# Attention keys in three chunks of 128, and the last 64 keys of two head pairs in one score tile (attention and gated MLP on one core)

## Chip, cores and metric

One Trainium2 chip, one core of it. The metric is the device time of one execution in microseconds (us): the median before the change is 725.34 us over 3 runs (722.62 to 725.93). A lower time is better. TensorE's clock has two levels, 1.2 and 2.4 GHz; the profile gives the share of the full one that was granted.

## What is computed

Eight batches, 12 heads of 64, 448 positions. Attention with a sigmoid in place of the softmax, then a gated MLP over 768 features with a product along the positions. Cut to what matters, the reference is:

```
scores = (q @ k.T) / sqrt(64) - log(448)
attn   = sigmoid(scores)
x      = attn @ v                       # heads side by side: (8, 448, 768)
h      = relu(x @ w_in)                 # (8, 448, 1024)
u, g   = h[..., :512], h[..., 512:]
g      = (g - mean(g)) / sqrt(var(g) + 1e-6)
g      = w_spatial @ g + b_spatial      # along the positions
out    = (u * g) @ w_out                # (8, 448, 768)
```

## The kernel before

**Units.** A unit is one batch and one pair of heads (`hp`, 6 per batch), so 48 units. Its q and k arrive as one tile `raw` of 128 partitions (two heads of 64) by 896 columns (448 of k, then 448 of q), its v as 4 chunks of 112 keys. `attention_splits` (L192) makes a high and a low part of `raw` in the tile `qks`: a cast and a subtraction, both on VectorE (DVE), L96 and L97.

**Scores.** A unit's 448 keys are 4 chunks of 112 (`KC`, `NC`). For each chunk `attention_scores` (L200) issues 3 terms (high by high, low by high, high by low) for the 2 heads: 6 matmuls (L207) with 64x112 stationary operands. The two heads lie in the upper and lower 64 rows of the array. ScalarE (ACT) then makes the sigmoid `at` of both heads at once (L212). A score tile takes one of 3 two-bank buffers of PSUM.

**Values.** `attention_values` (L217) multiplies a chunk of v by `at`: 2 matmul calls (L224), plain fp32, with 112x64 stationary operands, one for each head, side by side in the columns of the array. A call runs as two matmuls on the chip, so the profile counts 768 for 384 calls. The sums of a unit's 4 chunks stand in one bank `pav` (2 buffers). At the last chunk ACT copies `pav` to the high part of `x_s` (L96) and DVE makes the low part (L97).

**Order.** `attention(m)` (L372) runs through the 48 chunks of two batches in bursts of 3 (`BURST`): a burst's scores, then the values of the burst before, and so on: 16 bursts of either. The split of unit n+1 is issued ahead of chunk 1 of unit n, the loads of n+2 at chunk 0. Engines run their instructions in the program's order (`in_program_order`), as does the DMA queue of SyncE (SP).

**The rest of a stage.** There are 4 stages of two batches `b0`, `b1`. After the attention: `gate_values` four times (L239, matmuls `pv`), `spatial(b0)` twice (L291, `pg`), `gated(b0)` twice (L317, `pu`), `spatial(b1)` twice, `output(b0)` three times (L341, `po`), `gated(b1)` twice, `output(b1)` three times, between whose parts the first score burst of the next stage is placed. These matmuls are single-pass (fp32r) and write 448 or 512 columns.

**Weights.** In the first stage a generator (`weight_steps`, L136) loads and splits 22 pieces of weights beside the work: 6 of `w_in` (needed by `gate_values`), 4 of `w_sp`, 6 of `w_in` (needed by `gated`), 6 of `w_out` (needed by `output`). `load_weights(n)` runs n of its steps. A piece of `w_in` or `w_out` takes 3 steps (5 DVE operations) or, from piece `NFIRST` = 13 on, 4 steps (4 DVE operations and one more on ACT); then ACT copies the high part (L170) and POOL subtracts for the low part (L171). Attention runs a step after each chunk but chunk 1, from the third burst on; the calls behind `gate_values`, `spatial(b0)`, `gated(b0)` and `spatial(b1)` run `YB` = 4 each. `output` reads block 4 of `w_out` (piece 20) in the last quarter of its first column block.

Of the kernel before, what the change touches and what calls it, by code (L numbers as in the profile page):

```python
# [35 lines left out]
def attn_gmlp_kernel(  # L36
# [20 lines left out]

    nc = tc.nc  # L60
    B, NHP, _, _ = qk.shape
    KC, NC = v.shape[2:4]
    S = out.shape[3]
    D = P // 2
    NCC = out.shape[1]
    DM = NCC * P
    F = w_in.shape[1] // (4 * NCC)
    NFC = F // P
    HALF = 64
    NFULL = 3  # L70
    QK = 1.0 / math.sqrt(D)
    NEG_LOG_S = -math.log(S)
    NT = 2 * S // P
# [12 lines left out]
    x_s = const.tile([P, 2, NCC, 2 * S], F32R, name="x_s")  # L86
    bias_s = const.tile([P, 1], F32, name="bias_s")
# [48 lines left out]
    def weight_steps():  # L136
# [21 lines left out]
        for n, (src, dst, i) in enumerate(steps):  # L158
# [3 lines left out]
            hi, lo = dst[:, i, 0], dst[:, i, 1]  # L162
            scalar = n >= NFIRST
            val = raws.pop(n)
# [18 lines left out]
    loaded = {}  # L183

    def attention_loads(b, hp):
        raw = work.tile([P, 1024], F32, tag="raw", name=f"raw_{b}_{hp}", bufs=4)[:, : 2 * S]
        nc.sync.dma_start(raw, qk[b, hp])
        vt = work.tile([KC, NC, P], F32, tag="v", name=f"v_{b}_{hp}", bufs=4)
        nc.sync.dma_start(vt, v[b, hp])
        loaded[b, hp] = raw, vt  # L190

    def attention_splits(b, hp):  # L192
        raw, vt = loaded[b, hp]
        s = work.tile([P, 2, 2 * S], F32R, tag="split", name=f"qks_{b}_{hp}", bufs=3)
        split(s[:, 0], s[:, 1], raw, nc.vector.tensor_copy)
        loaded[b, hp] = s, vt

    TERMS = ((0, 0), (1, 0), (0, 1))

    def attention_scores(b, hp, c):  # L200
        s = loaded[b, hp][0]
        psc = banks(f"psc_{b}_{hp}_{c}")
        ks = slice(c * KC, (c + 1) * KC)
        for i, (a, e) in enumerate(TERMS):
            for j in range(2):
                rows = slice(j * D, (j + 1) * D)
                nc.tensor.matmul(  # L207
                    psc[:KC, j, :S], s[rows, a, ks], s[rows, e, S:], start=i == 0, stop=i == 2
                )
        at = work.tile([P, 2, 512], F32, tag="big", name=f"at_{b}_{hp}_{c}", bufs=7)  # L210
        at = at[:KC, :, :S]
        nc.scalar.activation(at, psc[:KC, :, :S], AF.Sigmoid, bias=bias_s[:KC], scale=QK)  # L212
        return at

    pav_of = {}

    def attention_values(b, hp, c, at):  # L217
        vt = loaded[b, hp][1]
        if c == 0:
            pav_of[b, hp] = ps_1.tile([P, 512], F32, tag="ps1", name=f"pav_{b}_{hp}")  # L220
        pav = pav_of[b, hp]
        for j in range(2):
            rows = slice(j * D, (j + 1) * D)
            nc.tensor.matmul(  # L224
                pav[rows, :S], vt[:, c, rows], at[:, j], start=c == 0, stop=c == NC - 1
            )
        if c == NC - 1:
            sl = slice((b % 2) * S, (b % 2 + 1) * S)
            split(x_s[:, 0, hp, sl], x_s[:, 1, hp, sl], pav[:, :S], nc.scalar.copy)
# [9 lines left out]
    def gate_values(m, ts):  # L239
# [51 lines left out]
    def spatial(b, fcs):  # L291

        odd = b % 2
        cols = cols_of(b)
        pg = banks(f"pg_{b}_{fcs[0]}")
        for i, fc in enumerate(fcs):
            fs = slice(fc * P, (fc + 1) * P)
            pairs = []
            for c in range(NFULL):
                vn = vns[c + 4 if odd else c]  # L300
                pairs.append(
                    (lambda a, vn=vn: vn[:, a, fs], lambda p, c=c: w_sp_s[:, c, p, cols])
                )
# [61 lines left out]
    BURST = 3  # L365
    units = [(b, hp) for b in range(B) for hp in range(NHP)]

    def ahead(f, n):
        if n < len(units):
            f(*units[n])  # L370

    def attention(m):  # L372

        chunks = [
            (b, hp, c) for b in (2 * m, 2 * m + 1) for hp in range(NHP) for c in range(NC)
        ]
        before = []
        for i in range(0, len(chunks) + BURST, BURST):
            now = []
            for b, hp, c in chunks[i : i + BURST]:  # L380
                n = b * NHP + hp
                if c == 0:
# [6 lines left out]
                now.append((b, hp, c, attention_scores(b, hp, c)))  # L389
# [9 lines left out]
    ahead(attention_loads, 0)  # L399
    ahead(attention_loads, 1)  # L400
    pairs = [(0, 1), (2, 3)]
    running = attention(0)
    for m in range(B // 2):
        for _ in running:
            pass
        for ts in ((0, 1), (2, 3), (4, 5), (6,)):
            gate_values(m, ts)
            load_weights(YB)
        b0, b1 = 2 * m, 2 * m + 1
        for fcs in pairs:  # L410
            spatial(b0, fcs)
            load_weights(YB)
# [6 lines left out]
        for n in range(2):  # L419
            ahead(attention_loads, (m + 1) * 2 * NHP + n)  # L420
# [61 lines left out]
```

## Time and profile before

| what | value |
|---|---|
| median of 3 runs (lowest, highest) | 725.34 us (722.62, 725.93) |
| the profiled execution's own time | 723.27 us |
| its span, first to last instruction | 721.5 us |
| granted TensorE clock, mean | 0.999 of full |
| TensorE matmul busy | 709.3 us, 98% |
| TensorE weight loads busy | 524.2 us, 73% |
| VectorE, ScalarE, GpSimd busy | 280.0, 274.1, 50.3 us |

Busy time of an engine is the union of its instructions. Matmuls are pipelined and their recorded ends are modelled, so a long busy time says that matmuls follow each other without a pause, not that the array is used in full. The chain of waits follows the last instruction back through whatever released each step; its rows give start, length, engine, tile and source line.

### The profile page before, as it was taken

What the parts mean: (1) busy time and instruction counts of PE and PEld (TensorE: products, weight loads), DVE (VectorE), ACT (ScalarE), POOL (GpSimd) and SP (SyncE); (2) the same over time, 40 slices, a digit from 0 to 9 for tenths busy, and PEclk for the clock granted to TensorE, in tenths of its full rate; (3) what the DMA queues carried; (4) which work ended last, traced back from release to release, by engine and by line L of the source; (5) the groups of instructions that cost most, each with busy time, mean ns of one, the idle gap of its engine ahead of it and who ended that gap; (6) DMA issues with size and microseconds to landing.
All of it is one profiled execution on the core that took longest, in us unless ns stands there. A gap on an engine that the chain in (4) does not pass through costs nothing.

```text
span 721.5 us, 9317 instructions
## 1 busy us (share of the span) xinstructions
PE 709.3 (98%) x3928; PEld 524.2 (73%) x3928; DVE 280.0 (39%) x423; ACT 274.1 (38%) x329; POOL 50.3 (7%) x58
## 2 busy tenths in 40 slices
PE   7999999999999999999999999999999999999997
PEld 4554689998755578999865557899985555889996
DVE  4977288703233226320233323722124332362110
ACT  5787322313477721011267771101137775101111
POOL 0333023200000001000000000100000000110000
PEclk9999999999999999999999999999999999999999
DMA  8648012221433200002143320000125320000102
GB/s 265 207 145 275 22 38 89 97 77 38 166 124 119 92 1 1 0 1 77 64 154 118 118 85 1 0 1 26 52 89 167 115 90 1 1 0 1 52 25 77
DMA packets 22938, 55.40 MB, mean 77 GB/s; under 512 B 2288, under 2 KB 8432, under 8 KB 22896
## 3 DMA queue, kind: packets, MB, share of 16 engines
q1 hardware_dynamic: 22896, 54.80, 22.8%
q8 instruction: 31, 0.51, 0.3%
q14 instruction: 11, 0.09, 0.0%
HBM read 43.78 MB, written 11.01 MB: 76 GB/s over the span
## 4 chain that ended last, share of the span: by engine, by line
PE 88%; DVE 2%; ACT 1%; issue 0%
PE pav L224 17%; PE pu L235 16%; PE pv L235 16%; PE po L235 15%; PE psc L207 14%; PE pg L235 10%; DVE gs L97 1%; DVE g L334 1%; ACT gs L96 1%; DVE qks L97 0%; ACT osb L362 0%; DVE wval L109 0%; DVE wval L125 0%; DVE wval L128 0%; DVE qks L96 0%
## 5 line engine op out<-in xcount | busy, mean ns | idle before, releaser
L212 ACT ACTIVATE at<-psc,bias_s 112x896 f32<-112x896 f32 x192 | 181.2, 1009 | 61.4 <-PE psc L207 60.9
L224 PE MATMUL pav<-at,v 112*64 112x448 f32 x768 | 157.6, 547 | 0.0
L207 PEld LDWEIGHTS psc<-qks 64*112 64x112 f32 x1152 | 98.6, 174 | 61.1 <-ACT at L212 17.6
L207 PE MATMUL psc<-qks 64*112 64x448 f32 x1152 | 136.9, 378 | 6.1 <-DVE qks L96 4.7
L235 PE MATMUL po<-gs,w_out_s 128*128 128x448 f32 x576 | 121.4, 369 | 1.6 <-DVE gs L97 1.6
L235 PE MATMUL pu<-x_s,w_in_s 128*128 128x448 f32 x576 | 118.0, 365 | 0.0
L235 PEld LDWEIGHTS po<-gs,w_out_s 128*128 128x128 f32 x576 | 107.4, 188 | 14.1 <-DVE gs L97 3.2
L235 PE MATMUL pv<-w_in_s,x_s 128*128 128x512 f32 x504 | 115.4, 390 | 0.0
L235 PEld LDWEIGHTS pu<-x_s,w_in_s 128*128 128x128 f32 x576 | 108.2, 188 | 8.6
L235 PEld LDWEIGHTS pv<-w_in_s,x_s 128*128 128x128 f32 x504 | 94.3, 188 | 22.3 <-issue 2.8
L224 PEld LDWEIGHTS pav<-at,v 112*64 112x64 f32 x768 | 49.8, 136 | 80.6 <-issue 78.9
L97 DVE TENSOR_TENSOR x_s<-pav,x_s 128x448 fp32r<-128x448 f32 x48 | 29.9, 624 | 147.5 <-ACT x_s L96 147.5
L235 PE MATMUL pg<-w_sp_s,vn 128*128 128x448 f32 x352 | 72.8, 365 | 0.0
L235 PEld LDWEIGHTS pg<-w_sp_s,vn 128*128 128x128 f32 x352 | 65.9, 187 | 5.8
L334 DVE SCALAR_TENSOR_TENSOR g<-pu,g 128x896 f32<-128x896 f32 x16 | 17.4, 1090 | 131.2 <-PE pu L235 131.2
L362 ACT COPY osb<-po 128x896 f32<-128x896 f32 x24 | 21.9, 911 | 116.5 <-PE po L235 116.5
L96 ACT CAST gs<-g 128x896 fp32r<-128x896 f32 x16 | 15.1, 945 | 127.2 <-DVE g L334 127.2
L97 DVE TENSOR_TENSOR qks<-raw,qks 128x896 fp32r<-128x896 f32 x48 | 53.4, 1112 | 1.6
L255 ACT ACTIVATE rv<-pv 128x1024 f32<-128x1024 f32 (+1 forms) x16 | 14.7, 920 | 83.5 <-PE pv L235 83.5
L96 DVE CAST qks<-raw 128x896 fp32r<-128x896 f32 x48 | 30.4, 633 | 40.8 <-PE po L235 34.8
L262 POOL TENSOR_SCALAR rstd<-mv 128x2 f32<-128x2 f32 (+1 forms) x16 | 6.4, 403 | 502.5 <-DVE mv L260 502.5
L259 DVE BATCH_NORM_STATS2 stats<-rv 128x6 f32<-128x512 f32 x28 | 19.0, 679 | 46.9 <-ACT rv L255 46.9
(29 smaller groups left out, 231.1 us busy)
## 6 DMA issues: line engine op xcount, KB each, us to landing
raw<-qk_dram SPq DMA_DIRECT2D x48, 448.0 KB, 4.1
v<-v_dram SPq DMA_DIRECT2D x48, 224.0 KB, 2.8
out_dram<-osb SPq DMA_DIRECT2D x24, 448.0 KB, 2.6
wraw<-w_in_dram SPq DMA_DIRECT2D x12, 512.0 KB, 4.9
wraw<-w_out_dram SPq DMA_DIRECT2D x6, 512.0 KB, 3.6
wraw<-w_sp_dram SPq DMA_DIRECT2D x4, 256.0 KB, 2.5
b_bc<-b_sp_dram SPq DMA_DIRECT2D x1, 256.0 KB, 3.3
```

The source lines that it names most:

```text
L96: copy(hi, src)
L97: nc.vector.tensor_sub(lo, src, hi.bitcast(F32))
L207: nc.tensor.matmul(psc[:KC, j, :S], s[rows, a, ks], s[rows, e, S:], start=i == 0, stop=i == 2)
L212: nc.scalar.activation(at, psc[:KC, :, :S], AF.Sigmoid, bias=bias_s[:KC], scale=QK)
L224: nc.tensor.matmul(pav[rows, :S], vt[:, c, rows], at[:, j], start=c == 0, stop=c == NC - 1)
L235: nc.tensor.matmul(ps, st, mv, start=start and i == 0, stop=stop and i == len(ops) - 1)
L255: nc.scalar.activation(rv[:, :n], pv[:, :n], AF.Relu)
L259: nc.vector.bn_stats(stats, rv[:, i])
L262: nc.gpsimd.tensor_scalar_add(rstd[:, :n], mv[:, :n, 1], 1e-6)
L334: nc.vector.scalar_tensor_tensor(g, pu[:, :, :S], 0.0, g, op0=ALU.max, op1=ALU.mult)
L362: nc.scalar.copy(osb, po[:, :, :S])
```

## The change

Keys are cut into 3 full chunks of 128 and one short one of 64. Two units (`hp` even and odd, a pair of units) share their short chunks: 7 score tiles (`t` = 0 to 6) in place of 8, of which `t` = 3 is the shared one, the even unit's keys in its upper 64 partitions and the odd unit's in its lower 64.

- The shared score tile takes 12 matmuls: 6 for each unit, with 64x128 stationary operands of which 64 columns are keys and 64 are zeros, so that both units' terms add up in one tile. For this `qks` gets 64 more columns, behind the 896 in an even unit and ahead of them in an odd one, which POOL sets to zero in each unit (a `memset` of 128x2x64, 48 in all). All other score matmuls are 64x128 as well.
- In the shared tile's values, 4 calls take 64x64 tiles: rows 0 to 63 (even unit) into one `pav`, rows 64 to 127 (odd unit) into the other. The other tiles take 128x64.
- v is loaded once for a pair of units, 128 partitions by 7x128, 2 buffers (before: each unit, 4 buffers).
- Splits: the odd unit's is issued ahead of `t` = 1, the next pair's even one ahead of `t` = 5.
- `NFIRST` is 11; a step of weights follows each tile but `t` = 1 and 5; `spatial(b1)` runs 8 steps each.

```
+    PART = 2 * S + HALF
-    NFIRST = NCC + NFC + 3
+    NFIRST = NCC + NFC + 1
...
     def attention_splits(b, hp):
+        s = work.tile([P, 2, PART], F32R, tag="split", name=f"qks_{b}_{hp}", bufs=3)
+        odd = hp % 2
+        zeros = s[:, :, :HALF] if odd else s[:, :, 2 * S :]
+        nc.gpsimd.memset(zeros.bitcast(F32), 0.0)
+        body = s[:, :, HALF:] if odd else s[:, :, : 2 * S]
+        split(body[:, 0], body[:, 1], raw, nc.vector.tensor_copy)
...
+    TILES = 2 * NFULL + 1
+    def attention_scores(b, hp, t):
+        for odd in range(2):
+            if t == NFULL or (t > NFULL) == odd:
+                full = 2 * HALF if odd else 0
+                k = (0 if odd else 2 * S - HALF) if t == NFULL else full + t % (NFULL + 1) * P
+                parts += [(loaded[b, hp + odd], k, full + NFULL * P, a, e) for a, e in TERMS]
...
     def attention_values(b, hp, t, at):
+        for odd in range(2):
+            if t == NFULL:
+                rows = slice(odd * HALF, (odd + 1) * HALF)
+            elif (t > NFULL) == odd:
+                rows = slice(0, P)
+            else:
+                continue
...
+            for j in range(2):
+                heads = slice(j * D, (j + 1) * D)
+                nc.tensor.matmul(pav[heads, :S], vt[rows, t, heads], at[rows, j], start=start, stop=stop)
...
     def attention(m):
-                if c == 0:
-                    if n % (2 * NHP) < 2 * NHP - 2:
-                        ahead(attention_loads, n + 2)
-                    if n % (2 * NHP) == 0:
-                        attention_splits(b, hp)
-                elif c == 1 and n % (2 * NHP) < 2 * NHP - 1:
-                    ahead(attention_splits, n + 1)
-                if m == 0 and i > BURST and c != 1:
+                if t == 1:
+                    ahead(attention_splits, n + 1)
+                if n + 2 < end:
+                    if t == 0:
+                        ahead(attention_loads, n + 2)
+                    elif t == NFULL:
+                        ahead(value_loads, n + 2)
+                        ahead(attention_loads, n + 3)
+                    elif t == 5:
+                        ahead(attention_splits, n + 2)
+                if m == 0 and i > BURST and t not in (1, 5):
                     load_weights(1)
...
         for fcs in pairs:
             spatial(b1, fcs)
-            load_weights(YB)
+            load_weights(2 * YB)
```

Three places show how instructions move. In the names, the figures behind a tile's name are unit or chunk and then a serial number; `x6` counts calls.

**Values on TensorE.** A burst of values before, three chunks of one unit:

```order
L224 MATMUL pav_2_262<-at_2_1_228,v_2_88 64x448 x2
L224 MATMUL pav_2_262<-at_2_2_237,v_2_88 64x448 x2
L224 MATMUL pav_2_262<-at_2_3_252,v_2_88 64x448 x2
```

The burst with a shared tile in its middle now, with the score bursts around it:

```order
L227 MATMUL psc_4_0_307<-qks_4_281 128x448 x6
L257 MATMUL pav_2_276<-at_2_2_232,v_2_121 64x448 x2
L257 MATMUL pav_2_276<-at_2_3_253,v_2_121 64x448 x2
L257 MATMUL pav_3_326<-at_2_3_253,v_2_121 64x448 x2
L257 MATMUL pav_3_326<-at_2_4_268,v_2_121 64x448 x2
L227 MATMUL psc_4_1_337<-qks_4_281 128x448 x6
```

The tile `at_2_3` is read by four calls, two into each `pav`; in other pairs of units it stands first or last in its burst.

**The split ahead of `t` = 5.** TensorE in the second stage now, a burst of values and the scores of tiles 5, 6 and the next pair's 0:

```order
L257 MATMUL pav_1_1668<-at_0_6_1640,v_0_1294 64x448 x2
L257 MATMUL pav_2_1718<-at_2_0_1651,v_2_1585 64x448 x2
L257 MATMUL pav_2_1718<-at_2_1_1664,v_2_1585 64x448 x2
L227 MATMUL psc_2_5_1727<-qks_3_1653 128x448 x6
L227 MATMUL psc_2_6_1736<-qks_3_1653 128x448 x6
L227 MATMUL psc_4_0_1747<-qks_4_1723 128x448 x6
```

VectorE there, the low part of the unit whose values that burst ends, then the split that the last of these score tiles reads:

```order
L100 TENSOR_TENSOR x_s<-pav_1_1668,x_s 128x448
L99 CAST qks_4_1723<-raw_4_1642 128x896
L100 TENSOR_TENSOR qks_4_1723<-raw_4_1642,qks_4_1723 128x896
```

Before, a unit's split was issued three chunks ahead of its first reader; now it is two tiles ahead.

**Weights beside `spatial(b1)`, first stage.** VectorE before (one piece, the last, between the two additions `g`):

```order
L312 TENSOR_TENSOR g_0_1278<-pg_0_1255,b_bc 128x2x448
L125 SCALAR_TENSOR_TENSOR wval_1252<-wraw_1152,wval_1252 128x512
L128 SCALAR_TENSOR_TENSOR wval_1252<-wraw_1152,wval_1252 128x512
L312 TENSOR_TENSOR g_2_1308<-pg_2_1285,b_bc 128x2x448
```

and now:

```order
L345 TENSOR_TENSOR g_0_1244<-pg_0_1221,b_bc 128x2x448
L128 SCALAR_TENSOR_TENSOR wval_1218<-wraw_1114,wval_1218 128x512
L131 SCALAR_TENSOR_TENSOR wval_1218<-wraw_1114,wval_1218 128x512
L112 TENSOR_SCALAR wval_1251<-wraw_1165 128x512
L119 TENSOR_SCALAR wraw_1165<-wraw_1165 128x512
L128 SCALAR_TENSOR_TENSOR wval_1251<-wraw_1165,wval_1251 128x512
L131 SCALAR_TENSOR_TENSOR wval_1251<-wraw_1165,wval_1251 128x512
L112 TENSOR_SCALAR wval_1259<-wraw_1216 128x512
L119 TENSOR_SCALAR wraw_1216<-wraw_1216 128x512
L345 TENSOR_TENSOR g_2_1285<-pg_2_1262,b_bc 128x2x448
L128 SCALAR_TENSOR_TENSOR wval_1259<-wraw_1216,wval_1259 128x512
L131 SCALAR_TENSOR_TENSOR wval_1259<-wraw_1216,wval_1259 128x512
```

The pieces are two later than before: 1218 is piece 19, 1251 piece 20 and 1259 piece 21. From `gate_values` to `gated(b0)` the number of steps between the kernel's own operations is what it was.

## Rows read from the trace of the kernel before

**Rows 1.** The page's first part: busy time of each engine, its share of the span, instructions.

```profile
PE 709.3 (98%) x3928; PEld 524.2 (73%) x3928; DVE 280.0 (39%) x423; ACT 274.1 (38%) x329; POOL 50.3 (7%) x58
```

**Rows 2.** The chain that ended last, share of the span by engine and line.

```profile
PE pav L224 17%; PE pu L235 16%; PE pv L235 16%; PE po L235 15%; PE psc L207 14%; PE pg L235 10%; DVE gs L97 1%; DVE g L334 1%; ACT gs L96 1%; DVE qks L97 0%; ACT osb L362 0%; DVE wval L109 0%; DVE wval L125 0%; DVE wval L128 0%; DVE qks L96 0%
```

**Rows 3.** Windows: the attention of the first three stages (in the later two without their first score burst). Start and end, length, then busy time of PE, PEld, DVE, ACT, POOL with instruction counts, granted clock, DMA share, GB/s.

```profile
4.70:80.16 75.46, 74.01 (x481) 38.39 (x481) 54.67 (x81) 57.50 (x72) 20.08 (x13) 1.00 0.64 207
188.46:257.09 68.63, 68.63 (x463) 35.18 (x463) 23.70 (x32) 48.37 (x57) 0.00 (x0) 1.00 0.36 118
365.39:434.02 68.63, 68.63 (x464) 35.19 (x463) 23.70 (x32) 48.37 (x57) 0.00 (x0) 1.00 0.36 118
```

**Rows 4.** The chain in order of time, third stage: start, length, what. The last score burst stands between two bursts of values; the two last bursts of values follow each other.

```profile
398.39 2.41 PE pav L224 x12
400.79 2.02 PE psc L207 x18
402.81 2.41 PE pav L224 x12
...
429.36 4.66 PE pav L224 x24
434.02 28.79 PE pv L235 x126
```

**Rows 5.** Groups of instructions by line and shape: line, engine, operation, tiles, shapes, count, then busy us and mean ns of one, then idle time before.

```profile
L212 ACT ACTIVATE at<-psc,bias_s 112x896 f32<-112x896 f32 x192 | 181.2, 1009 | 61.4 <-PE psc L207 60.9
L207 PEld LDWEIGHTS psc<-qks 64*112 64x112 f32 x1152 | 98.6, 174 | 61.1 <-ACT at L212 17.6 <-ACT x_s L96 16.9 <-DVE qks L96 4.7
L235 PEld LDWEIGHTS pu<-x_s,w_in_s 128*128 128x128 f32 x576 | 108.2, 188 | 8.6
L224 PE MATMUL pav<-at,v 112*64 112x448 f32 x768 | 157.6, 547 | 0.0
L171 POOL TENSOR_TENSOR w_in_s<-wval,w_in_s 128x512 fp32r<-128x512 f32 x12 | 18.8, 1570 | 70.5 <-ACT w_in_s L170 70.5
L466 POOL MEMSET const-float32-0.0<- 128x1 f32 x1 | 0.1, 98 | 0.2 <-issue 0.2
```

**Rows 6.** Weight loads in order of time, three narrow windows in one score burst: start, length, tile, shape, how many at once.

```profile
401.02 0.17 PEld L207 LDWEIGHTS psc<-qks 64*112 64x112 f32 x2
401.23 0.17 PEld L207 LDWEIGHTS psc<-qks 64*112 64x112 f32 x2
401.43 0.18 PEld L207 LDWEIGHTS psc<-qks 64*112 64x112 f32 x2
```

**Rows 7.** ACT and DVE in order of time around the same score burst: start, length, operation, idle time before and who ended it.

```profile
400.84 0.53 ACT L96 CAST x_s<-pav 128x448 fp32r<-128x448 f32 x1 [0.77 <-PE pav L224]
401.69 2.81 ACT L212 ACTIVATE at<-psc,bias_s 112x896 f32<-112x896 f32 x3 [0.32 <-PE psc L207]
...
401.40 0.62 DVE L97 TENSOR_TENSOR x_s<-pav,x_s 128x448 fp32r<-128x448 f32 x1 [2.89 <-ACT x_s L96]
401.95 0.62 DVE L96 CAST qks<-raw 128x896 fp32r<-128x896 f32 x1
402.60 1.09 DVE L97 TENSOR_TENSOR qks<-raw,qks 128x896 fp32r<-128x896 f32 x1
```

**Rows 8.** The chain in order of time in the first stage, a piece of weights and a split on DVE ahead of a score burst.

```profile
68.00 0.69 DVE wval L128
68.69 0.55 DVE qks L96
...
69.27 1.10 DVE qks L97
...
70.42 0.66 PE psc L207 x4
```

**Rows 9.** First stage around `spatial(b1)`: the chain's pieces of TensorE, then DVE, ACT and POOL in order of time.

```profile
141.42 14.78 PE po L235 x72
...
138.72 1.09 DVE L312 TENSOR_TENSOR g<-pg,b_bc 128x896 f32<-128x896 f32 x1
139.72 0.86 DVE L125 SCALAR_TENSOR_TENSOR wval<-wraw,wval 128x512 uint32<-128x512 uint32 x1
140.61 0.69 DVE L128 SCALAR_TENSOR_TENSOR wval<-wraw,wval 128x512 uint32<-128x512 uint32 x1
141.45 1.09 DVE L312 TENSOR_TENSOR g<-pg,b_bc 128x896 f32<-128x896 f32 x1
...
138.88 0.69 ACT L118 ACTIVATE wraw<-wraw 128x512 f32<-128x512 f32 x1 [0.23 <-DVE wraw L116]
141.34 0.62 ACT L170 CAST w_out_s<-wval 128x512 fp32r<-128x512 f32 x1 [1.77 <-DVE wval L128]
...
142.04 1.29 POOL L171 TENSOR_TENSOR w_out_s<-wval,w_out_s 128x512 fp32r<-128x512 f32 x1 [2.01 <-ACT w_out_s L170]
```

**Rows 10.** DVE at the start of the program, and the DMA issues (KB each, median us from issue to landing).

```profile
4.00 0.63 DVE L96 CAST qks<-raw 128x896 fp32r<-128x896 f32 x1 [3.11 <-DMA raw<-qk_dram]
7.82 0.63 DVE L96 CAST qks<-raw 128x896 fp32r<-128x896 f32 x1 [2.07 <-DMA raw<-qk_dram]
...
raw<-qk_dram SPq DMA_DIRECT2D x48, 448.0 KB, 4.1
v<-v_dram SPq DMA_DIRECT2D x48, 224.0 KB, 2.8
```

More of the change, by code (lines that the diff above doesn't have):

```diff
@@ L61, in attn_gmlp_kernel @@
     B, NHP, _, _ = qk.shape
-    KC, NC = v.shape[2:4]
     S = out.shape[3]
@@ L183, in attn_gmlp_kernel @@
     loaded = {}
+    values = {}
     def attention_loads(b, hp):
@@ L187, in attention_loads, with value_loads @@
         nc.sync.dma_start(raw, qk[b, hp])
-        vt = work.tile([KC, NC, P], F32, tag="v", name=f"v_{b}_{hp}", bufs=4)
-        nc.sync.dma_start(vt, v[b, hp])
-        loaded[b, hp] = raw, vt
-    def attention_splits(b, hp):
[L193 to L196, printed above, removed]
-    TERMS = ((0, 0), (1, 0), (0, 1))
[L200 to L204, printed above, removed]
+        loaded[b, hp] = raw
+    def value_loads(b, hp):
+        vt = work.tile([P, 2 * NFULL + 1, P], F32, tag="v", name=f"v_{b}_{hp}", bufs=2)
+        nc.sync.dma_start(vt, v[b, hp // 2])
+        values[b, hp] = vt
+    def attention_splits(b, hp):
+        raw = loaded[b, hp]
+        s = work.tile([P, 2, PART], F32R, tag="split", name=f"qks_{b}_{hp}", bufs=3)
[4 more added lines that the diff above has]
+        split(body[:, 0], body[:, 1], raw, nc.vector.tensor_copy)
+        loaded[b, hp] = s
+    TERMS = ((0, 0), (1, 0), (0, 1))
+    TILES = 2 * NFULL + 1
+    def attention_scores(b, hp, t):
+        psc = banks(f"psc_{b}_{hp}_{t}")
+        parts = []
+        for odd in range(2):
[3 more added lines that the diff above has]
+                parts += [(loaded[b, hp + odd], k, full + NFULL * P, a, e) for a, e in TERMS]
+        for i, (s, k, q, a, e) in enumerate(parts):
             for j in range(2):
@@ L207, in attention_scores @@
                 nc.tensor.matmul(
-                    psc[:KC, j, :S], s[rows, a, ks], s[rows, e, S:], start=i == 0, stop=i == 2
-                )
-        at = work.tile([P, 2, 512], F32, tag="big", name=f"at_{b}_{hp}_{c}", bufs=7)
-        at = at[:KC, :, :S]
-        nc.scalar.activation(at, psc[:KC, :, :S], AF.Sigmoid, bias=bias_s[:KC], scale=QK)
+                    psc[:, j, :S],
+                    s[rows, a, k : k + P],
+                    s[rows, e, q : q + S],
+                    start=i == 0,
@@ L213, in attention_scores, with attention_values @@
+                    stop=i == len(parts) - 1,
+                )
+        at = work.tile([P, 2, 512], F32, tag="big", name=f"at_{b}_{hp}_{t}", bufs=7)[:, :, :S]
+        nc.scalar.activation(at, psc[:, :, :S], AF.Sigmoid, bias=bias_s, scale=QK)
         return at
     pav_of = {}
-    def attention_values(b, hp, c, at):
-        vt = loaded[b, hp][1]
-        if c == 0:
[L220 to L229, printed above, removed]
+    def attention_values(b, hp, t, at):
+        vt = values[b, hp]
+        for odd in range(2):
[5 more added lines that the diff above has]
+                continue
+            unit = b, hp + odd
+            start = t == odd * NFULL
+            stop = t == (1 + odd) * NFULL
+            if start:
+                pav_of[unit] = ps_1.tile([P, 512], F32, tag="ps1", name=f"pav_{b}_{hp + odd}")
+            pav = pav_of[unit]
+            for j in range(2):
+                heads = slice(j * D, (j + 1) * D)
+                nc.tensor.matmul(pav[heads, :S], vt[rows, t, heads], at[rows, j], start=start, stop=stop)
+        for odd in range(2):
+            if t == (1 + odd) * NFULL:
+                sl = slice((b % 2) * S, (b % 2 + 1) * S)
+                x = x_s[:, :, hp + odd, sl]
+                split(x[:, 0], x[:, 1], pav_of.pop((b, hp + odd))[:, :S], nc.scalar.copy)
@@ L370, in ahead, with start_loads @@
             f(*units[n])
+    def start_loads(m):
+        n = m * 2 * NHP
+        ahead(attention_loads, n)
+        ahead(value_loads, n)
+        ahead(attention_loads, n + 1)
     def attention(m):
-        chunks = [
-            (b, hp, c) for b in (2 * m, 2 * m + 1) for hp in range(NHP) for c in range(NC)
-        ]
+        first, end = 2 * NHP * m, 2 * NHP * (m + 1)
+        tiles = [(n, t) for n in range(first, end, 2) for t in range(TILES)]
         before = []
-        for i in range(0, len(chunks) + BURST, BURST):
+        for i in range(0, len(tiles) + BURST, BURST):
             now = []
-            for b, hp, c in chunks[i : i + BURST]:
-                n = b * NHP + hp
-                if c == 0:
-                    if n % (2 * NHP) < 2 * NHP - 2:
-                        ahead(attention_loads, n + 2)
-                    if n % (2 * NHP) == 0:
-                        attention_splits(b, hp)
-                elif c == 1 and n % (2 * NHP) < 2 * NHP - 1:
-                    ahead(attention_splits, n + 1)
-                now.append((b, hp, c, attention_scores(b, hp, c)))
-                if m == 0 and i > BURST and c != 1:
+            for n, t in tiles[i : i + BURST]:
+                if n == first and t == 0:
+                    ahead(attention_splits, n)
+                if t == 1:
+                    ahead(attention_splits, n + 1)
+                if n + 2 < end:
+                    if t == 0:
+                        ahead(attention_loads, n + 2)
+                    elif t == NFULL:
[3 more added lines that the diff above has]
+                        ahead(attention_splits, n + 2)
+                now.append((*units[n], t, attention_scores(*units[n], t)))
+                if m == 0 and i > BURST and t not in (1, 5):
                     load_weights(1)
@@ L397, in attention @@
             yield
-    ahead(attention_loads, 0)
-    ahead(attention_loads, 1)
+    start_loads(0)
     pairs = [(0, 1), (2, 3)]
@@ L417, in attn_gmlp_kernel @@
             spatial(b1, fcs)
-            load_weights(YB)
-        for n in range(2):
-            ahead(attention_loads, (m + 1) * 2 * NHP + n)
+            load_weights(2 * YB)
+        start_loads(m + 1)
         output(b0, (0, 1))
@@ L446 @@
     H0 = S - 64
-    KC = 112
     q = q.copy()
     q[1::2] = np.concatenate([q[1::2, :, H0:], q[1::2, :, :H0]], axis=2)
-    qk = np.concatenate([k, q], axis=2)
+    full, short = k[:, :, :H0], k[:, :, H0:]
+    qk = np.concatenate([full, q, short], axis=2)
+    qk[:, 2::4] = np.concatenate([short, full, q], axis=2)[:, 2::4]
+    qk[:, 3::4] = np.concatenate([short, full, q], axis=2)[:, 3::4]
     qk = np.ascontiguousarray(np.transpose(qk, (0, 1, 3, 2))).reshape(B, H // 2, 2 * D, 2 * S)
-    vT = v.reshape(B, H // 2, 2, S // KC, KC, D)
-    vT = np.ascontiguousarray(np.transpose(vT, (0, 1, 4, 3, 2, 5)))
-    vT = vT.reshape(B, H // 2, KC, S // KC, 2 * D)
+    vT = np.transpose(v.reshape(B, H // 4, 2, 2, S, D), (0, 1, 4, 2, 3, 5)).reshape(B, H // 4, S, 2, 2 * D)
+    full = np.transpose(vT[:, :, :H0].reshape(B, H // 4, 3, P, 2, 2 * D), (0, 1, 3, 4, 2, 5))
+    short = np.transpose(vT[:, :, H0:], (0, 1, 3, 2, 4)).reshape(B, H // 4, P, 1, 2 * D)
+    vT = np.concatenate([full[:, :, :, 0], short, full[:, :, :, 1]], axis=3)
+    vT = np.ascontiguousarray(vT)
     w_in = np.transpose(moe_w_in.reshape(DM // P, P, 2, F), (1, 2, 0, 3)).reshape(P, -1)
```

## Prediction

> **What bounds the kernel now.** I read busy times first, then the chain of waits by line, then windows by stage, then single bursts in order of time. TensorE has matmuls in flight for 98% of the span [rows 1], and the chain runs through it for 88%: values L224 17%, scores L207 14%, the rest the MLP's products [rows 2]. In the windows of attention TensorE is never idle in the later stages (68.63 of 68.63 us) while ACT works 48.4 us and DVE 23.7 [rows 3]. So a matmul slot that goes is worth its whole length, and ACT's 24 fewer sigmoids of 1.009 us [rows 5] are worth nothing by themselves: ACT waits for the scores.
>
> Prices of a slot: 24 value matmuls in one piece take 4.66 us, 12 take 2.41 [rows 4]. The difference, 2.25 us for 12, is six pairs of 0.375 us; the remaining 0.16 us is paid once a burst, on changing from and to the scores' tile shape. A pair runs at once: 12 matmuls of 547 ns on average [rows 5] fit into 2.41 us. A chunk's values (2 calls, 4 matmuls) are two slots, 0.75 us. Score pairs follow each other at 0.205 us [rows 6]; nine make 1.85 of a burst's 2.02 us [rows 4], so 0.17 us is paid per burst there.
>
> **What the change removes.**
> - Values: per pair of units 7 tiles for 8 chunks, if the four 64x64 calls run side by side. 24 x 0.75 = **-18.0 us**.
> - Bursts: 42 tiles in bursts of 3 are 14, not 16, of either kind; 8 fewer in all, each 0.16 + 0.17: **-2.6 us**.
> - Scores: 6 x 3 + 6 terms are 24, as 8 x 3 were: no gain. The stationary operand grows from 112 to 128 columns. Its load took 174 ns, that of a 128x128 operand 188 ns [rows 5], both under the slot of 205 ns: no cost. Bounds 0 and 14 ns x 576 = 8 us; I take 0, as the 128-column products keep the same slot (14.78 us for 72 [rows 9]).
>
> **What it adds.**
> - Tile shapes. The shared tile changes from 128x64 to 64x64 tiles and back. It stands first, second or last in a burst by turns; at a burst's edge one of the two changes is there already. That leaves 1 + 2 + 1 extra for three pairs of units, 8 a stage, 32 in all. No row shows this change; the nearest are the 0.16 and 0.17 us of a burst, which pay for two changes of shape with unhidden loads. A single one, with its first slot unhidden, may come near the whole; I take 0.16: **+5.1 us**, bounds 0 and 6. The Trainium skill (TensorEngine Tiling (Array Packing), Key Properties) says that a change of tiling mode drains the engine; by that the lower bound is out, and the bursts' 0.16 us agree.
> - Splits. Two a stage are now close to their reader. From the start of ACT's cast of `pav` to the end of the split's subtraction it takes 2.85 us, 400.84 to 403.69 [rows 7]. In bursts [5, 6, 0], starting at T, the burst of scores before had the shared tile (2.02 + 3 x 0.205 = 2.63 us), so ACT's sigmoids run later and its cast starts near T - 1.0; the low keys are there at T + 1.85. Tile 0's second term wants them at T + 0.17 + 7 x 0.205 = T + 1.60, its load a slot earlier: a wait of about 0.4. In bursts [1, 2, 3] the cast waits for the shared tile in the values' middle (T - 0.8), ready at T + 2.05, wanted at T + 2.0 to 2.2: 0.15. Two of each a stage: 1.1 us, in three stages **+3.3**, bounds 0 and 6.
> - First stage. It takes 75.46 us against 68.63 + 2.02 = 70.65 later [rows 3, 4], partly slow start, partly DVE: a split behind a piece of weights that holds TensorE stands in the chain [rows 8]. The pieces (five operations, near 3 us) now stand between closer splits, about 0.7 us at each of four places; some of that is paid already. Also the first v (448 KB, not 224) lies ahead of the second `raw`, which landed at 7.8 [rows 10]; its reader comes late enough but for some 0.3 us. Net **+1.3**, bounds -1.8 and +5.
> - `w_out`. From `gate_values` to `gated(b0)` DVE's order is the same with pieces two later, so the times [rows 9] hold up to piece 19's last operation (141.31). Then piece 20: two operations (142.2), ACT's multiplication 0.69 (142.9), two operations of 0.86 and 0.69 (144.5), ACT's copy 0.62 (145.2), POOL's low part 1.29 (146.6). `po` starts at 141.42 and reads block 4 with its tenth matmul, 143.3. High part then low part are late: **+3.0 us**, once; bounds 0 and 4. Before, piece 20 was over by 140.
> - Zeros: 48 memsets of 128x2x64 on POOL, which has 50 us of work in 721 [rows 1]. Price between 0.1 us (128x1) and 1.6 (128x512 subtraction) [rows 5]; each stands two tiles or more ahead of its reader: 0. Without that cover a shared tile would wait for it, and behind POOL's weights in the first stage.
> - v: half the issues, same bytes; tiles 0 and following have some 8 us, against 2.8 to 4.1 to land [rows 10]: 0. SP waits for the v buffer of two pairs before, whose last reader is at most a burst away.
>
> **Sum.** -18.0 - 2.6 + 5.1 + 3.3 + 1.3 + 3.0 = -7.9 us. Against the profiled execution's 723.27 that is 715.4; the median of the runs lies 2.1 us above it, which gives 717.4. I forecast **716**, between the two.
>
> **Rivals.**
> 1. *Three slots for the shared tile.* A call's two passes stand behind each other in the program, so four calls are eight matmuls of which the second of each must wait for its first. If the engine can look past only the calls of one half, the lower half's first passes start with the upper half's second ones: three slots, 24 x 0.375 = +9.0 us, 725. For it: nothing here shows four tiles at once. Against it: twelve matmuls take six slots with no seventh [rows 4], so a blocked pass does not hold the other column's. The Trainium skill (TensorE: Matmul & The Clock Gate, Part 3: Packing small matmuls, What overlaps and what doesn't) has matmuls strictly in program order; by that the forecast would be 725, and the trace speaks against it as far as two calls go. Chance 0.13.
> 2. *The halves one after the other* (the other side). If fp32 passes of the upper and the lower rows do not overlap, a shared tile takes four slots, as two chunks did, and all that was added stays: 24 x 0.75 = +18 us, 734, slower. It decides from the point at which a shared tile exceeds about 1.08 us (0.75 + 7.9/24). Against it: score pairs in upper and lower rows load two at once and keep 0.205 us [rows 6], though in one pass. Chance 0.10.
> 3. *No new wait shows.* Splits and piece 20 come in time (DVE is idle for two thirds of a stage): 716 - 3.3 - 1.3 - 3.0, about 708. Chance 0.15.
> 4. *DVE becomes the bound.* Each of 16 close splits costs 1 us and more rather than 0.3: +8 to +12, 724 to 728. Chance 0.07.
> The forecast's case: 0.55, alone 711 to 720.
>
> **Numbers.** A measurement can tell about 0.5%, 3.6 us. Faster than 721.7: forecast, rival 3 and a little of 1 and 4, 0.71. Within: most of 1, part of 4, 0.16. Slower than 729: rival 2 and the end of 4, 0.13. The range 707 to 726 holds the forecast's case, rivals 3 and 1 and half of 4, some 8 in 10.
>
> **What would show it.** Right: windows of attention of about 66 us in place of 68.63; value bursts of 2.41 without and 2.55 to 2.75 with a shared tile; score bursts of 2.02 and 2.63, those of [5, 6, 0] some 0.4 longer, their idle time ended by DVE `qks`; in the first stage the first `po` piece 3 us longer, waiting for `w_out_s` from ACT and POOL. Wrong: bursts with a shared tile of 3.1 (rival 1) or 3.5 us (rival 2); score slots above 0.205; waits ended by POOL `qks`.

## The result, and the profile after

The changed kernel takes **728.88 us** (median; 727.64 to 729.57) against 723.34 of the kernel before on the same chip: a ratio of **1.0062, 95% interval 1.0038 to 1.0087**. It is slower by 5.5 us, where 716 was forecast from a median of 725.34. The profiled execution has a span of 727.1 us against 721.5, so its difference of 5.6 can be followed in the trace.

The page's first part, with the shares of the chain by engine under it, answers to [rows 1]:

```profile
PE 704.0 (97%) x3928; PEld 524.0 (72%) x3928; DVE 278.6 (38%) x421; ACT 254.6 (35%) x307; POOL 57.5 (8%) x106
PE 83%; DVE 8%; ACT 4%; issue 2%; DMA 2%; POOL 1%; SPq 0%; ACTq 0%
```

The chain by engine before the change:

```profile
PE 88%; DVE 2%; ACT 1%; issue 0%
```

TensorE is busy for 5.3 us less, yet its share of the chain fell from 88% to 83%, and DVE, ACT, DMA and POOL gained. So work was saved and waits took its place. Where they are, the windows show (columns as in [rows 3]): attention of the first two stages, then the first stage's `pu` of b0 and the first `po`.

```profile
4.63:82.21 77.58, 72.10 (x481) 37.81 (x481) 47.70 (x71) 50.84 (x64) 16.31 (x20) 0.98 0.52 186
201.83:267.82 65.99, 65.64 (x464) 34.15 (x463) 23.97 (x32) 43.24 (x51) 2.25 (x10) 1.00 0.37 126
119.94:141.63 21.69, 17.86 (x73) 15.00 (x72) 13.98 (x22) 5.37 (x8) 5.61 (x5) 0.84 0.31 94
150.44:169.39 18.95, 16.84 (x74) 14.73 (x72) 4.91 (x8) 4.42 (x6) 3.80 (x3) 0.91 0.22 74
```

Against [rows 3] the second attention takes 2.64 us less, the third and fourth 2.6 as well (66.02 and 66.02 us), -7.9 in all. The first takes 2.1 more. `pu` takes 7.1 more than the 14.59 us it takes in the second stage, `po` 4.2 more than its 14.78 [rows 9]. That is +2.1 + 7.1 + 4.2 - 7.9 = +5.5: everything lost was lost once, in the first stage, where the weights are converted.

The chain in the third stage answers to [rows 4].

```profile
383.25 2.57 PE pav L257 x16
...
391.50 1.10 DVE qks L100
...
393.31 2.72 PE pav L257 x16
396.02 2.71 PE psc L227 x24
398.74 2.41 PE pav L257 x12
```

A burst of values with the shared tile takes 2.57 us at a burst's edge and 2.72 in its middle, and 2.41 without: two slots for four calls, and 0.16 us a change of shape, as forecast. The first of these bursts shows the four calls at once: their first passes begin together, and their second passes 0.42 us later (two narrow windows, as in [rows 6]).

```profile
383.19 0.61 PE L257 MATMUL pav<-at,v 64*64 64x448 f32 x4
383.61 0.56 PE L257 MATMUL pav<-at,v 64*64 64x448 f32 x4
```

The burst of scores [5, 6, 0] waits for the split; it takes 2.46 us (390.78 to 393.24 by PE's own rows) against 2.02:

```profile
390.78 1.69 PE L227 MATMUL psc<-qks 64*128 64x448 f32 x14
392.64 0.66 PE L227 MATMUL psc<-qks 64*128 64x448 f32 x4 [0.17 <-DVE qks L100]
393.24 2.79 PE L257 MATMUL pav<-at,v 128*64 128x448 f32 x16
```

What `pu` waited for: PE and POOL in order of time (start, length, operation, idle time before and who ended it).

```profile
119.94 2.59 PE L268 MATMUL pu<-x_s,w_in_s 128*128 128x448 f32 x12
123.75 0.48 PE L268 MATMUL pu<-x_s,w_in_s 128*128 128x448 f32 x1 [1.22 <-ACT w_in_s L173]
125.11 0.82 PE L268 MATMUL pu<-x_s,w_in_s 128*128 128x448 f32 x2 [0.89 <-POOL w_in_s L174]
127.04 0.74 PE L268 MATMUL pu<-x_s,w_in_s 128*128 128x448 f32 x1 [1.10 <-ACT w_in_s L173]
128.40 13.40 PE L268 MATMUL pu<-x_s,w_in_s 128*128 128x448 f32 x56 [0.62 <-POOL w_in_s L174]
```

```profile
123.77 1.28 POOL L174 TENSOR_TENSOR w_in_s<-wval,w_in_s 128x512 fp32r<-128x512 f32 x1 [3.37 <-ACT w_in_s L173]
127.06 1.28 POOL L174 TENSOR_TENSOR w_in_s<-wval,w_in_s 128x512 fp32r<-128x512 f32 x1 [2.00 <-ACT w_in_s L173]
```

These are the last two pieces of `w_in`, 14 and 15. In the kernel before, POOL's row of the last one stood here:

```profile
115.66 1.29 POOL L171 TENSOR_TENSOR w_in_s<-wval,w_in_s 128x512 fp32r<-128x512 f32 x1 [4.55 <-ACT w_in_s L170]
```

It was over at 116.95, 1.1 us before `pu` began at 118.03 and some 4.3 us before `pu`'s 17th matmul, the first that reads it (16 slots of 0.203 us). Now it is over at 128.34, 11.4 us later, while `pu` begins only 1.9 us later, at 119.94: the 17th matmul starts about 5.2 us late. In all the idle times are 3.8 us; the other 3.3 us are matmuls at a lower clock, part of them between the waits and part behind them. Four windows (granted clock third from the end): the waits of `pu`, what follows them, and what follows the waits of `po` and of the first attention.

```profile
122.53:128.40 5.87, 2.04 (x5) 0.78 (x5) 5.77 (x10) 2.60 (x4) 2.56 (x2) 0.75 0.45 121
128.40:131.50 3.10, 3.10 (x8) 2.83 (x9) 1.95 (x4) 0.62 (x1) 1.15 (x1) 0.50 0.50 159
156.30:160.00 3.70, 3.70 (x13) 3.32 (x12) 0.00 (x0) 0.85 (x2) 1.28 (x1) 0.55 0.00 0
71.28:75.19 3.91, 3.91 (x14) 1.17 (x14) 1.95 (x4) 1.54 (x2) 0.00 (x0) 0.62 0.44 134
```

And the first attention's chain towards its end:

```profile
56.49 0.33 SPq L196
...
57.39 0.38 SPq L157
...
58.34 8.35 DMA wraw<-w_sp_dram
...
66.71 0.03 ACT w_sp_s L173
...
67.23 0.54 ACT x_s L99
...
68.33 0.97 DVE qks L99
...
69.33 1.10 DVE qks L100
...
70.47 0.80 PE psc L227 x4
71.28 3.91 PE pav L257 x12
```

Read from below: scores wait for a split on DVE, which stands behind the split of `pav`, whose cast on ACT stands behind the copy of a spatial weight that lands only at 66.69. SyncE had issued `raw` at 46.32 and then stood at the `v` (L196) until 56.49, with two pieces of weights and the bias behind it.

### The profile page after: what moved, and what is told of

Same layout as the page of the kernel before. It is cut to its first block, busy times and chain, and to the rows that moved or that the text cites. A ratio compares the mean times of both kernels' runs of the same rounds, so it can differ in the third digit from the quotient of the medians.

```text
span 727.1 us, 9370 instructions
## 1 busy us (share of the span) xinstructions
PE 704.0 (97%) x3928; PEld 524.0 (72%) x3928; DVE 278.6 (38%) x421; ACT 254.6 (35%) x307; POOL 57.5 (8%) x106
## 3 DMA queue, kind: packets, MB, share of 16 engines
q1 hardware_dynamic: 20208, 54.80, 21.7%
## 4 chain that ended last, share of the span: by engine, by line
PE 83%; DVE 8%; ACT 4%; issue 2%; DMA 2%; POOL 1%; SPq 0%; ACTq 0%
PE pav L257 17%; PE pu L268 16%; PE psc L227 15%; PE po L268 15%; PE pv L268 13%; PE pg L268 7%; ACT at L235 2%; DVE qks L100 1%; DMA wraw<-w_sp_dram 1%; DVE vn L309 1%; DVE qks L99 1%; DVE wval L128 1%; DVE g L367 1%; DVE gs L100 1%; ACT gs L99 1%
## 5 line engine op out<-in xcount | busy, mean ns | idle before, releaser
L235 ACT ACTIVATE at<-psc,bias_s 128x896 f32<-128x896 f32 x168 | 159.8, 1007 | 66.5 <-PE psc L227 66.3
L227 PE MATMUL psc<-qks 64*128 64x448 f32 x1152 | 137.8, 380 | 11.1 <-DVE qks L99 8.2
L227 PEld LDWEIGHTS psc<-qks 64*128 64x128 f32 x1152 | 104.5, 187 | 59.2 <-ACT x_s L99 21.1
L257 PE MATMUL pav<-at,v 128*64 128x448 f32 (+1 forms) x768 | 144.9, 557 | 0.0
L268 PE MATMUL po<-gs,w_out_s 128*128 128x448 f32 x576 | 123.5, 372 | 3.8 <-DVE gs L100 1.7
L268 PE MATMUL pu<-x_s,w_in_s 128*128 128x448 f32 x576 | 121.3, 370 | 3.8 <-ACT w_in_s L173 2.3
L257 PEld LDWEIGHTS pav<-at,v 128*64 128x64 f32 (+1 forms) x768 | 41.0, 136 | 79.7 <-issue 78.8
L268 PE MATMUL pg<-w_sp_s,vn 128*128 128x448 f32 x352 | 72.8, 365 | 0.0
L395 ACT COPY osb<-po 128x896 f32<-128x896 f32 x24 | 21.8, 909 | 114.8 <-PE po L268 114.8
L206 POOL MEMSET qks<- 128x128 f32 x48 | 10.5, 223 | 330.7 <-PE po L268 192.3
```

The lines of the kernel that those rows point to most:

```text
L206: nc.gpsimd.memset(zeros.bitcast(F32), 0.0)
L227: nc.tensor.matmul(psc[:, j, :S], s[rows, a, k : k + P], s[rows, e, q : q + S], start=i == 0, stop=i == len(parts) - 1,)
L235: nc.scalar.activation(at, psc[:, :, :S], AF.Sigmoid, bias=bias_s, scale=QK)
L257: nc.tensor.matmul(pav[heads, :S], vt[rows, t, heads], at[rows, j], start=start, stop=stop)
L395: nc.scalar.copy(osb, po[:, :, :S])
```

## The experiments

The theories: **A**, the pace of the weights (26 steps in the first attention instead of 32, so two pieces fall behind) costs the gain; **C**, `v` with two buffers holds SyncE's queue and so the first attention; **B**, VectorE has no room anyway; later ones beside their runs. Times in us; "first" and "third" are the attentions of those stages (the third without its first score burst, as in [rows 3]), "between" is from the first attention's end to the start of the second one's window, all read from the matmuls of the profiled execution. The ratios are against the kernel before, run beside each on the same chip; its median was 723.33 to 723.85. The executions of one kernel differ, those of the change from 727.64 to 729.57, and "first" carries about 1 us of that: the first value burst began 7.1 us after the first matmul in the change and 7.9 in e1, whose edit comes only behind the attention.

| run | median | ratio to before, 95% | first | between | third |
|---|---|---|---|---|---|
| before | 723.34 | 1 | 75.4 | 108.3 | 68.6 |
| the change | 728.88 | 1.0062, 1.0038 to 1.0087 | 77.6 | 119.6 | 66.0 |
| e1 two pieces behind gate values | 723.53 | 0.9997, 0.9988 to 1.0006 | 76.2 | 115.4 | 66.0 |
| e2 `v` late | 723.63 | 0.9995, 0.9986 to 1.0005 | 72.9 | 119.3 | 66.0 |
| e3 both | 719.29 | 0.9929, 0.9908 to 0.9951 | 72.9 | 114.8 | 66.0 |
| e4 before, 25 steps | 744.10 | 1.0282, 1.0266 to 1.0297 | 73.0 | 133.1 | 68.6 |
| e5 pace of before | 714.63 | 0.9876, 0.9861 to 0.9891 | 74.9 | 108.3 | 65.9 |
| e6 e5 and `v` late | 714.45 | 0.9876, 0.9861 to 0.9890 | 75.0 | 108.3 | 66.0 |
| e7 e6 and split early | 709.42 | 0.9804, 0.9787 to 0.9820 | 72.5 | 108.3 | 65.1 |
| e8 before, 26 steps | 731.59 | 1.0110, 1.0095 to 1.0125 | 72.8 | 119.8 | 68.6 |
| e9 e5 and split early (but for the first pair) | 712.24 | 0.9847, 0.9831 to 0.9864 | 74.6 | 108.3 | 65.1 |
| e10 e9, other order of calls | 712.13 (one run) | | 74.9 | 108.3 | 65.1 |
| e11 e9, 128 rows | 720.67 (one run) | | 74.8 | 108.3 | 68.0 |

### e1: two pieces behind the first gate values

```diff
             gate_values(m, ts)
-            load_weights(YB)
+            load_weights(2 * YB if ts[0] < 4 else YB)
```

Expected: 

> The changed kernel, in which the first two pairs of tiles of the gate values carry two pieces of weights each instead of one, so that the pieces catch up with the kernel before. Theory A (the later weights cost the gain): pu of batch 0 no longer waits for w_in_s (21.70 us back to 14.6) and the first po no longer for w_out_s (18.95 back to 14.8), so 728.9 - 11.3 = 717.6 us; the first attention stays at 77.4 us. Rival B (VectorE has no room for two pieces behind one pair of gate values, so the delay only moves into pv and pg): under half of it, 723 to 729 us.

As B says, under half of the 11.3 us came back: `po` is at 14.78 us again, but PE now waits ahead of it, in `pg` and ahead of `pu`:

```profile
109.48 4.69 PE L268 MATMUL pg<-w_sp_s,vn 128*128 128x448 f32 x22
115.40 4.70 PE L268 MATMUL pg<-w_sp_s,vn 128*128 128x448 f32 x22 [1.23 <-ACT rv L288]
123.44 1.88 PE L268 MATMUL pu<-x_s,w_in_s 128*128 128x448 f32 x5 [3.35 <-ACT rv L288]
```

`rv` on ACT, which frees the PSUM that they want, stands behind ACT's copy of a piece (L173), and that waited for VectorE. "Between" gave back 4.2 us of the 11.3, the rest moved: B holds behind the gate values. Another 1.4 us came in the first attention, which the edit does not touch; why is not shown.

### e2: `v` issued at t = 6

```diff
                     elif t == NFULL:
-                        ahead(value_loads, n + 2)
                         ahead(attention_loads, n + 3)
...
+                    elif t == 6:
+                        ahead(value_loads, n + 2)
```

Expected: 

> The changed kernel, in which the v of the next pair is issued at the pair's last tile (t = 6), not at the shared one (t = 3), so that SyncE's queue does not stand at it. Theory C (the first attention loses its gain because v with two buffers holds the queue and with it the spatial weights behind it until 56.5 us): the waits of 1.3, 3.0 and 0.8 us in the last bursts of the first attention go in the main, its end comes some 4 us earlier, 725 us in all; what follows stays as long. Rival D (the pieces come late because fewer steps of weights are taken in the first attention, and SyncE's queue waits for their buffers anyway): 0 to -1 us, 728 to 729.

C holds here, and the gain is near the forecast one: the first attention takes 4.7 us less and what follows as long as before (`pu` 21.4, `po` 19.0). SyncE in order of time:

```profile
52.49 0.33 SPq L157 DMA_DIRECT2D wraw<-w_sp_dram  x1
...
58.81 0.33 SPq L157 DMA_DIRECT2D wraw<-w_sp_dram  x1
59.24 0.38 SPq L196 DMA_DIRECT2D v<-v_dram  x1
```

The piece that went out at 57.39 leaves at 52.49, and ACT's copies of the last two (61.32 and 63.71 us) no longer wait for a DMA.

### e3: both

The edits of e1 and e2 together.

Expected: 

> Both edits, two pieces behind the first gate values and v issued at t = 6. If A and C hold and do not share a cause, the gains add: 728.9 - 11.3 - 4 = 713.6 us. If C falls, 717.6 as with the first edit alone.

The gains add: 4.7 us in the first attention, as in e2, and 4.9 behind it, where e1 gave 4.2. It falls short of 713.6 by what e1 fell short of 11.3.

### e4 and e8: the kernel before, with late weights

```diff
-    NFIRST = NCC + NFC + 3
+    NFIRST = NCC + NFC + 1
...
-                if m == 0 and i > BURST and c != 1:
+                if m == 0 and i > 4 * BURST and c != 1:
...
             spatial(b1, fcs)
-            load_weights(YB)
+            load_weights(2 * YB)
```

Expected: 

> The kernel before, with nothing of the new tiles, but two pieces of weights fewer in the first attention (its steps of weights begin three bursts later and two pieces change to the form in which ScalarE multiplies). Theory A: pu and po of the first stage wait as in the changed kernel, 723.3 + 11.3 = 734.6 us less what the first attention saves by carrying less, 0 to 2 us: 732.5 to 734.6. Rival E (the lateness does harm only together with the closer splits and the v buffers of the change): 723 to 726 us.

Slower as A says, and E falls, but by 20.3 us where 9 to 11 were expected: "between" grew by 24.8 in the profiled execution, which at 745.45 us is the slowest of the four. A piece in the form with ScalarE's multiplication has four steps. Behind 25 steps, the next group of four steps is one whole piece; behind 26 it is the second half of one piece and the first half of the next. One thing that DVE waited for in e4 from 104 to 150 us (us in total, times, longest), and a window beside `pu`:

```profile
DVE wval L125 <- ACT wraw L118: 4.5, 6, 0.8
...
120.00:130.00 10.00, 5.06 (x12) 3.10 (x10) 7.78 (x12) 2.21 (x4) 1.78 (x2) 0.50 0.20 57
```

VectorE stands inside each piece until ACT has multiplied; the pieces around `pu` end 5 us apart. Behind the longer waits TensorE had half its clock for these 10 us, which is part of the loss. So e8 adds one step:

```diff
         for _ in running:
             pass
+        if m == 0:
+            load_weights(1)
```

Expected: 

> The kernel before with late weights again, now with one step more behind the last values, 26 as the change takes, so that VectorE stands at the same half of a piece when the gate values begin. Theory A with F (the half piece is worth much, as VectorE then has not to wait for ScalarE's multiplication inside a piece): pu 21 to 23 and po 18 to 20 us, pg as it was, 723.3 + 11.3 - 2.7 (a first attention that carries less ended 2.7 us earlier) = 732 us. Rival: the step is nothing, 744 us as with 25.

731.59 where 732 was expected, and PE has the rows of the changed kernel, lengths and idle times within 0.2 us:

```profile
119.14 0.47 PE L235 MATMUL pu<-x_s,w_in_s 128*128 128x448 f32 x1 [1.22 <-ACT w_in_s L170]
...
122.42 0.74 PE L235 MATMUL pu<-x_s,w_in_s 128*128 128x448 f32 x1 [1.25 <-ACT w_in_s L170]
123.78 13.57 PE L235 MATMUL pu<-x_s,w_in_s 128*128 128x448 f32 x56 [0.61 <-POOL w_in_s L171]
```

None of the new tiles is in this kernel: late weights alone cost what was lost between the attentions, 11.5 us here and 11.3 there. From 92 to 145 us DVE never waits for ACT inside a piece. "Late" is two things at once in e4, e5 and e8, the number of steps and the form of two pieces (`NFIRST`); no run separates them.

### e5 and e6: the pace of before

```diff
-                if m == 0 and i > BURST and t not in (1, 5):
+                if m == 0 and i > BURST and t != 1:
...
-    NFIRST = NCC + NFC + 1
+    NFIRST = NCC + NFC + 3
```

and the step of e8 behind the last values, 32 in all.

Expected: 

> The changed kernel with the weights' pace of the kernel before: 32 steps of weights in the first attention instead of 26 (beside every tile but t = 1, and one behind the last values), so 13 pieces and the start of the next, the first 13 in the form without ScalarE's multiplication. Theory A: pu back to 14.6 and po to 14.8 us, and pg not lengthened as it was by two pieces behind the gate values; the first attention carries two more pieces and its tile-by-tile waits grow by 0 to 3 us: 717.6 to 721 us. Rival B (VectorE is full wherever the two pieces go): what pu and po give back the first attention takes, 725 to 729.

714.63 us, better than expected, since the first attention did not grow but fell to 74.9 us. `pu` and `po` stand in the chain as in the kernel before:

```profile
117.38 14.59 PE pu L268 x72
...
140.77 14.78 PE po L268 x72
```

Expected of e6, with e2's edit on top: 

> The same with v issued at t = 6. Theory A and C together: the 4.7 us that the late v gave in the first attention come on top, 713 to 716 us. Rival B: 719 to 724.

714.45: the late `v` is worth nothing here. The time lies in the range of A and C by luck, since e5 was already there. With the split at `t` = 5, C is not a cause of its own: `v` in the queue does harm when pieces that are wanted at once stand behind it, and at the old pace the spatial weights had been issued earlier (at 44.65 to 52.53 us in e5).

### e7 and e9: the split one burst earlier

```diff
-                    elif t == 5:
+                    elif t == 4:
                         ahead(attention_splits, n + 2)
```

Expected: 

> The same, and the split of the next pair's first unit is issued at t = 4 instead of t = 5, one burst earlier. Theory G (what is left of the close splits is VectorE's queue, not the shared tile): in the three later stages the two score bursts [5, 6, 0] come down from 2.47 to 2.05 us, 6 x 0.43 = 2.6 us less than without. Rival: the split then stands ahead of the split of pav and makes that late, nothing gained, 0 us.

5.0 us less than e6, where 2.6 were expected. The windows of e7:

```profile
4.64:77.10 72.46, 70.95 (x481) 38.32 (x481) 53.25 (x79) 51.73 (x66) 20.70 (x22) 1.00 0.62 214
185.44:250.45 65.01, 65.01 (x463) 34.35 (x463) 23.87 (x32) 43.22 (x51) 2.24 (x10) 1.00 0.37 128
```

In the later stages TensorE is never idle again, and 0.9 us a stage is what G said. The other 2.5 us came in the first attention, which had not been counted on: there the split at `t` = 5 also stood behind the pieces of weights. About 1.6 us of that was clock: behind e6's wait a burst of values with the shared tile in its middle took 4.29 us in place of 2.72, at a granted clock of 0.61, while e7's is 1.00 in both windows. This is the fastest kernel, 13.9 us below the one before.

e9 is e7 with `v` at t = 3 and the very first pair's split at t = 5.

Expected: 

> The changed kernel with the pace of weights of before (32 steps, 13 pieces) and the split of the next pair's first unit at t = 4 (in the very first pair still at t = 5), but v issued where the change has it. Theory A': with the pieces at their old pace the place of v is worth nothing, so the time is that with the late v or 0.9 us less, 708.5 to 710 us. Rival C: without the late v the close of the first attention waits again, 713 us.

712.24: here C has an effect after all, 2.1 us in the first attention, nowhere else. The first pair's split has no part in this loss: from the first value burst to 58 us e9 stands 0.8 us ahead of e7 at every burst, and at the attention's end 2.1 behind. The chain shows a piece of `w_in` on its way, the split behind it, and a burst of values of 3.54 us in place of 2.41:

```profile
58.31 6.09 DMA wraw<-w_in_dram
...
64.45 0.44 DVE wraw L123
...
68.70 3.54 PE pav L257 x12
```

It left behind `v` and `raw`, which SyncE issued from 56.66 on; in e7, where `v` leaves at 59.48, behind it, the step L123 of DVE began at 62.77, 1.7 us earlier. In e6 the landing of an earlier piece (issued at 54.80) set the chain, so the place of `v` did not show there.

### e10 and e11: the four calls of the shared tile

Both are edits of e9. e10 runs both units' first head, then both units' second head (a sort of the same four calls).

Expected: 

> The same kernel with the four 64x64 calls of the shared tile in the other order: both units' first head, then both units' second head, so that calls behind one another lie in the two row halves and not in the two column halves. If four calls run at once in any order, value bursts with a shared tile stay at 2.57 us (at an edge) and 2.72 (in the middle). Rival: TensorE pairs only neighbouring calls of different columns, or looks past only one call: 2.9 to 3.5 us.

The chain, second stage:

```profile
194.98 2.57 PE pav L258 x16
...
204.60 2.72 PE pav L258 x16
```

Nothing changes: four 64x64 calls take two slots in either order. e11 leaves out the 64-row tiles:

```diff
             if t == NFULL:
-                rows = slice(odd * HALF, (odd + 1) * HALF)
+                rows = slice(0, P)
```

Expected of e11: 

> The same kernel with the four calls of the shared tile over all 128 rows, in 128x64 tiles like the other values, in place of 64x64 (each unit then also adds the other unit's 64 keys, a part of the computation that is changed on purpose to leave the tile shape alone). If the shared tile's gain is that its two row halves run side by side, the four calls take four slots of 0.375 us: 2.41 + 0.75 = 3.16 us in all bursts with a shared tile, with no change of shape; 24 shared tiles x (0.75 - 0.16 or 0.31, 0.21 on average over first, middle and last) = 12.9 us more. Rival: the calls still take two slots, 2.41 us, and the whole gain is in the smaller number of tiles.

```profile
194.87 3.16 PE pav L257 x16
...
205.08 3.16 PE pav L257 x16
```

3.16 us at the edge and in the middle, 2.41 + 0.75, as expected: the two halves side by side are the gain. The time rose by 8.4 us, not 12.9: 2.9 in each later stage, but 0.2 in the first, where TensorE does not set the pace; and the [1, 2, 3] bursts gave back the 0.08 us that they waited.

## Why the prediction was wrong, point by point

- **Values, bursts, scores, tile shapes: right.** Two slots for the shared tile, 0.16 us per change of shape, 18 score slots in 2.02 and 24 in 2.63 us. Rivals 1 and 2 are out (3.1 and 3.5 us did not come; e10, e11).
- **Close splits: right.** 0.44 us in each [5, 6, 0] burst (0.4 forecast) and 0.08 in [1, 2, 3] (0.15). With all this a later attention came to 66.0 us, as forecast (65.9); e7 gets 0.9 of it back.
- **The failing step was the term `w_out`**: "From `gate_values` to `gated(b0)` DVE's order is the same with pieces two later, so the times [rows 9] hold up to piece 19's last operation". From there I followed only what `po` reads. Two pieces later also means that `w_in`'s pieces 14 and 15 come behind the gate values, and `pu` reads them: the last one had been done some 4.3 us before the matmul that wants it, and it came 11.4 us later. `pu` lost 7.1 us, for which the sum had no term. e8 shows it without the new tiles, e5 takes it away.
- **The same term's size: 4.2 us for 3.0.** 2.1 of them are idle time, less than forecast; the other 2.1 are the lower clock behind it, for which the sum had no term.
- **First attention: +2.1 where -2.6 were forecast** (a quarter of the three terms on tiles, -3.9, and +1.3). The step on `v` failed: "SP waits for the v buffer of two pairs before, whose last reader is at most a burst away". The reader was near; but SyncE runs ahead of TensorE, so it stood there for 9.7 us with the spatial weights behind it. e2 gave back 4.7 us. e5 shows the other half of the cause: with the old pace the queue's wait does no harm until the split moves. And the +1.3 for closer splits behind pieces was too small: with the old pace the attention still took 74.9 us, 0.5 less than before, and the earlier split took 2.5 off (e7).
- **The sum.** 7.1 + 1.2 + 4.7 us account for 13.0 of the 13.5 by which -7.9 missed +5.6; the rest is 0.15 us a later stage. With the pace undone e5 measures 714.6, near the 716 forecast, but that is in part luck: the +3.0 for `w_out` is then gone, and the first attention gains 0.5 us where 2.6 were forecast.
- Rival 4 (724 to 728) came near the time by another road: it had DVE as the bound at the splits, which cost 0.44 and 0.08 us in the later stages. That weights end late for `pu` was in no rival.

How much of the first attention is bound by ACT and how much by DVE was not separated. e7's 72.5 us against 65.1 later holds the first score burst, which the later windows leave out, a slow start and waits behind pieces. The slow start is 8.0 us for the first two score bursts, where later ones take 2.0 and 2.6: their pairs follow each other at 0.37 us until about 11 us, in the changed kernel until 9.4 us, and then at 0.205. The granted clock in the rows is 1.00 there, so the cause stays open.

## What to carry to other kernels

When an edit shortens a stage, ask what else was paced by its steps: background work that is handed out per tile gets fewer turns, and everything that reads its result must be checked for slack, the next reader first. A load that waits for a buffer in an in-order queue costs what stands behind it, not what it loads. Where TensorE waits several times close together, add the clock that may fall behind it: in `pu` and `po` here it cost about as much as the waits.

## What the runs showed of the hardware

- **Several waits of about 1 us close together cost as much again in clock.** From 122.5 to 128.4 us TensorE had five matmuls in flight for 2.0 us; behind that the granted clock was 0.50 (1.2 of 2.4 GHz) for 3.1 us, in which 8 matmuls began where 15 would have at `pu`'s usual 0.203 us. The windows behind the waits of `po` (0.55) and of the first attention (0.62) show the same, and e8's `pu` has the same mean of 0.84. Not every wait does it: behind e1's single wait of 1.23 us the clock was 1.00, behind its 3.35 us `pu` took 16.5 us in place of 14.6, and the later attentions with their waits of 0.2 us have 1.00. The Trainium skill (TensorE: Matmul & The Clock Gate, Part 1: The HAM clock gate) says "the default state is throttled, and activity releases the throttle"; the rows agree so far that the clock fell where matmuls paused and came back while they ran.
- **Four 64x64 tiles of fp32 calls run at once whichever way the calls are ordered** (2.57 us in e10 as in the changed kernel; there four begin at 383.19 and four at 383.61). The Trainium skill (TensorEngine Tiling (Array Packing), Tiling Modes) lists 64x64 as four independent tiles; the trace agrees, with 0.16 us for each change from and to 128x64.
- **One step of weights more is worth 12 us** (20.3 above the kernel before in e4, 8.3 in e8): the two differ by two VectorE operations ahead of the gate values. With a whole piece in a group DVE waited six times for ACT's multiplication, 4.5 us in all, and the pieces ended 4.9 us apart in place of 3.3; the rest is waits that follow from it and the clock (0.50 from 120 to 130 us), not separated.
